# Pooled attention and a GELU MLP on one core: denominators ahead of outputs in the first batch, the last row tile in column parts, and one store per row tile

## The chip, the cores and the metric

The kernel runs on one core of a Trainium2 chip. The metric is the device time of one execution in microseconds (us), lower is better. A profiled execution gives a page and a trace; times inside it are counted from the start of the span.

## The reference

```python
def _attn_ref(q, k, v):                      # 8 batches, 8 heads, 576 rows, 64 columns
    k_p = k.reshape(B, H, Sp, 8, D).mean(axis=3)      # Sp = 72
    v_p = v.reshape(B, H, Sp, 8, D).mean(axis=3)
    scores = scale * np.matmul(q, k_p.transpose(0, 1, 3, 2))
    attn = softmax(scores)
    return np.matmul(attn, v_p)
# heads side by side: x has 4608 rows of 512
h = x @ w_in                                 # 512 -> 2048
g = gelu_tanh(h)
out = g @ w_out                              # 2048 -> 512, float32
```

Keys and values are averaged over eight neighbouring rows, each query row attends over the 72 averaged ones, and a two-layer MLP with a tanh GELU follows.

## The kernel before, in words

**Groups.** The MLP works on nine groups g of 512 rows of x, which is held transposed in xT (128 partitions, 4 slices of the model dimension, 4608 columns). In each group the up-projection `p1_mm` (L336) makes 16 tiles of 128 hidden units by 512 rows in PSUM banks, four matmuls per tile, `gelu` (L342) turns each into a part of gT, and the down-projection `p2_mm` (L345) makes four row tiles of 128 output rows from 16 matmuls each. `store` (L350, L356) copies a row tile from PSUM to an osb buffer (six of them) on VectorE and writes it to memory.

**Order.** The schedule is written by hand: each engine runs its instructions in the order of the program text, and waits are put in where data or buffers demand them. While the group g is in its down-projection, the attention of batch g+1 is woven into it at fixed places (`pos`, in matmuls of the down-projection): `qk` (L239) makes scores, `expo` (L247) their exponentials, `av` (L261) outputs and denominators, `norm` (L268 to L271) reciprocals by a logarithm and an exponential, and `mult` (L279) writes xT. In the up-projection of group g stand the sums for batch g+1: `k_steps` and `v_steps` (L139) on VectorE, the transposes of k (L174), and `v_moves` (L152), two small DMAs on SP's queue that move pooled rows of v from kp to vp.

**Loads.** `load_next` (in group g, for batch g+2) issues the q load on POOL's queue, a DMA transpose of q on SP's queue (L224), then a one-element copy `gate` on POOL (L448) that waits for the transpose, and behind it on POOL the loads of k and v. The weights w_in_b and w_out_b are loaded once; w_out_b in four parts of four hidden blocks fo each, on POOL's queue (L113), behind the loads of batch 1.

**The first batch** has no down-projection to hide in. It stands alone at the start, with steps of its own: `den0` (L289) makes the denominators of two pairs of heads by matmuls with a constant, `inverse0` (L294, L296) their reciprocals into rc0 (two buffers), `av0` (L304) the outputs of two pairs, and `mult0` (L308) their product into xT. c is the half of the rows and pr the first pair of heads. `spin` (L362) issues matmuls of zeros whose results nobody reads. The end of that stage, with PSUM banks as last arguments:

```python
    spin(4, 4)
    av0(0, 0, 4); mult0(0, 0, 4)
    den0(0, 2, 2); inverse0(0, 2, 2)
    av0(1, 0, 0); mult0(1, 0, 0)
    spin(3, 6)
    den0(1, 2, 6); inverse0(1, 2, 6)
    spin(3, 4)
    av0(0, 2, 4); mult0(0, 2, 4)
    spin(3, 0)
    av0(1, 2, 0); mult0(1, 2, 0)
```

Behind it comes the up-projection of group 0, its first eight matmuls on slices 0 and 1 of xT, then those on slices 2 and 3.

**Stores.** The rows of the output that a row tile holds are spread: each run of 32 columns of xT belongs to one of 18 positions within a stride of 18 rows. Each row tile is therefore written by four DMAs of 32 rows of 2 KB, all from SP's queue; the very last row tile uses SP's and ACT's queues in turn. SP's queue in a group holds, in order, the transpose of q, the two moves into vp, and the sixteen stores.

Of the kernel before, what the change touches and what calls it, by code (L numbers as in the profile page):

```python
# [8 lines left out]
F32 = mybir.dt.float32  # L9
# [9 lines left out]
def kernel(  # L19
# [9 lines left out]
    nc = tc.nc  # L29
    B, H, S, D = q.shape  # L30
    Sp = S // 8
    N = B * S
    DM = H * D
    DF = moe_w_in.shape[1]
    KO = DM // 128
    FO = DF // 128
    T = S // 32
    TP = T // 2
    CH = S // 2
    GROUP = 512  # L40
    NG = N // GROUP
# [11 lines left out]
    opool = ctx.enter_context(tc.tile_pool(name="op", bufs=6))  # L53
# [4 lines left out]
    PS = psp.tile([128, 8, 512], F32, name="PS")  # L58
# [19 lines left out]
    def load_v(b, engs):  # L78
        rows = v[b].rearrange("h (j l) d -> j h (l d)", l=8)
        for i in range(2):  # L80
            engs[i % len(engs)].dma_start(out=vts[b % 2][64 * i:64 * i + 64], in_=rows[0:64, 4 * i:4 * i + 4])  # L81

    def load_q(b, i0=0, i1=2):
        if b not in qs:
            qs[b] = qp.tile([128, 2, T * D], BF16, name="qb")
        nc.gpsimd.dma_start(  # L86
            out=qs[b][:, i0:i1],
            in_=q[b].rearrange("(i h) (p t) d -> (h p) i (t d)", i=2, t=T)[:, i0:i1])
# [3 lines left out]
    w_out_b = consts.tile([128, FO, DM], BF16, name="w_out_b")  # L92
# [104 lines left out]
    def trans_k(b, bank):  # L197
        trans_k_mm(b, bank)
        for e in range(2):
            trans_k_copy(b, e, bank)  # L200
# [21 lines left out]
    def trans_q_dma(b):  # L222
        qTs[b] = bp.tile([128, 2, TP, 128], BF16, name="qT")
        nc.sync.dma_start_transpose(out=qTs[b].rearrange("p i t c -> p (i t) c"),  # L224
                                    in_=qs[b].rearrange("p i c -> p (i c)"))
# [6 lines left out]
    def pool_rows(pr):  # L232
        return Sp if pr < PR // 2 else 128
# [49 lines left out]
    def den0(c, pr, bank):  # L283
        for x in range(2):
            e = es[0, c, pr + x]
            n = pool_rows(pr)
            for y in range(2):
                one = ones[:n, pr // 2].rearrange("j a d -> j (a d)")[:, 64 - 64 * y:192 - 64 * y]
                nc.tensor.matmul(out=PS[:, bank + x, :CH], lhsT=one, rhs=e[:n, y, :],  # L289
                                 start=(y == 0), stop=(y == 1))  # L290

    def inverse0(c, pr, bank):
        ld = ep.tile([128, 2, CH], F32, name="ld0", bufs=1)
        nc.scalar.activation(out=ld, in_=PS[:, bank:bank + 2, :CH], func=ACT.Ln)  # L294
        rc = ep.tile([128, 2, CH], F32, name="rc0")
        nc.scalar.activation(out=rc, in_=ld, func=ACT.Exp, scale=-1.0)  # L296
        rcs[0, c, pr] = rc

    def av0(c, pr, bank):
        for x in range(2):  # L300
            e = es.pop((0, c, pr + x))
            n = pool_rows(pr)
            for y in range(2):
                nc.tensor.matmul(out=PS[:, bank + x, :CH], lhsT=window(vz[:n], 2 * (pr + x) + y),  # L304
                                 rhs=e[:n, y, :], start=(y == 0), stop=(y == 1))

    def mult0(c, pr, bank):
        nc.vector.tensor_tensor(out=xT[:, pr:pr + 2, c * CH:(c + 1) * CH], in0=PS[:, bank:bank + 2, :CH],  # L308
                                in1=rcs.pop((0, c, pr)), op=ALU.mult)
# [3 lines left out]
    def act_set(name):  # L313
        nc.scalar.preload_act_table_set(name)  # L314


    def x_bank(g):
        return g % 2
# [9 lines left out]
    def o_bank(g, r):  # L328
        return 1 - x_bank(g) if r % 2 == 0 else x_bank(g)

    gTs = {}
# [9 lines left out]
            gTs[g] = gpool.tile([128, FO, GROUP], BF16, name="gT")  # L341
        nc.scalar.activation(out=gTs[g][:, fo, :], in_=PS[:, h_bank(g, fo), :], func=ACT.Gelu_apprx_tanh)  # L342

    def p2_mm(g, r, fo):
        nc.tensor.matmul(out=PS[:, o_bank(g, r), :], lhsT=gTs[g][:, fo, r * 128:(r + 1) * 128], rhs=w_out_b[:, fo, :],  # L345
                         start=(fo == 0), stop=(fo == FO - 1))

    def store(g, r):
        osb = opool.tile([128, DM], F32, name="osb")
        nc.vector.tensor_copy(out=osb, in_=PS[:, o_bank(g, r), :])  # L350

        for n in range(4):
            b, c = divmod(g * GROUP + r * 128 + n * 32, S)
            rows = out[b * S:(b + 1) * S].rearrange("(p t e) d -> e t p d", t=TP, e=2)
            eng = nc.scalar if (g, r) == (NG - 1, 3) and n % 2 else nc.sync
            eng.dma_start(out=rows[c // CH, c % CH // 32], in_=osb[n * 32:(n + 1) * 32, :])  # L356


    def spin(n, bank):

        for _ in range(n):
            nc.tensor.matmul(out=PS[:, bank, :], lhsT=idle[:, 0:128], rhs=idle, start=True, stop=True)  # L362
# [24 lines left out]
    for h in range(H):  # L387
        i = h // 4
        nc.tensor.matmul(out=PS[64 - 64 * i:72 - 64 * i, 7, h * D:(h + 1) * D],
                         lhsT=identb[0:64, 32 * i + h % 4:32 * i + 32:4], rhs=kps[0][0:64, KR],  # L390
                         start=True, stop=True)
# [3 lines left out]
    for i in range(2):  # L395
        p = slice(64 - 64 * i, 72 - 64 * i)
        nc.vector.tensor_copy(out=vz[p, 4 * i:4 * i + 4, 0],
                              in_=PS[p, 7, 256 * i:256 * i + 256].rearrange("p (h d) -> p h d", d=D))
# [9 lines left out]
    for f in v_steps(0):  # L408
        f()
    inverse0(1, 0, 6)  # L410
    spin(4, 4)
    av0(0, 0, 4)
    mult0(0, 0, 4)
    den0(0, 2, 2)
    inverse0(0, 2, 2)
    av0(1, 0, 0)
    mult0(1, 0, 0)
    spin(3, 6)
    den0(1, 2, 6)
    inverse0(1, 2, 6)  # L420
    spin(3, 4)
    av0(0, 2, 4)
    mult0(0, 2, 4)
    spin(3, 0)
    av0(1, 2, 0)
    mult0(1, 2, 0)
    for t in kps:
# [12 lines left out]
    for g in range(NG):  # L440
        nb = g + 1 if g + 1 < B else None
        act_set(GELU_SET)

        def load_next():

            load_q(g + 2)
            trans_q_dma(g + 2)
            nc.gpsimd.tensor_copy(out=gate, in_=qTs[g + 2][0:1, 1, TP - 1, 0:2])  # L448
            load_k(g + 2, [nc.gpsimd])
            load_v(g + 2, [nc.gpsimd])  # L450

        if 0 < g and g + 2 < B:
            load_next()


        side = {fo: [] for fo in range(FO)}
        if nb is not None:
            kk = k_steps(nb)
            tk = [lambda: trans_k(nb, 4)]
            kk.append(lambda: v_moves(nb))  # L460
            vv = v_steps(nb)
            if g:
                plan = {2: kk[:1], 3: kk[1:], 7: vv[:1], 8: vv[1:], 9: tk}
            else:
                tq = [lambda a=a, i=i: trans_q(nb, *a, (5, 6, 7, 5)[i], nc.vector) for i, a in enumerate(QG)]
                plan = {0: kk, 12: tq[:1], 13: tq[1:2] + tk, 14: tq[2:3], 15: tq[3:] + vv}
            for fo, what in plan.items():
                side[fo] += what

        if g == 0:
            first = [(fo, ko) for ko in (2, 3) for fo in range(4)]
        else:
            late = 3
            rest = [fo for fo in range(4) if fo != late]
            first = [(fo, ko) for ko in range(3) for fo in rest]
            first += [(late, ko) for ko in range(3)]
            first += [(fo, 3) for fo in rest + [late]]
        for fo, ko in first:  # L480
            p1_mm(g, fo, ko)
        for fo in range(FO):
            if fo >= 4:
                for ko in range(KO):
                    p1_mm(g, fo, ko)
            gelu(g, fo)
            for s in side[fo]:
                s()

        if g == 0:  # L490
            load_next()


        todo = {}

        def at(m, f, *a):
            todo.setdefault(m, []).append((f, a))

        if nb is not None:
            act_set(EXP_SET)  # L500
            pos = (6, 14, 20, 27, 34, 41, 48, 55, 61)
            for i in range(len(ORDER) + 1):
                if i < len(ORDER):
                    at(pos[i], qk, nb, *ORDER[i], 2)
                if i:
                    a = (nb, *ORDER[i - 1], 4 + 2 * ((i - 1) % 2))
                    at(pos[i], av, *a)
                if i < len(ORDER):
                    at(pos[i], expo, nb, *ORDER[i], 2)
                if i:  # L510
                    at(pos[i], norm, *a)
                    at(min(pos[i] + 9, 62 if i < len(ORDER) else 65), mult, *a)
        seq = [(r, fo) for r in range(4) for fo in range(FO)]
        if g == 0:

            seq[:32] = [(r, 4 * f4 + f) for f4 in range(4) for r in range(2) for f in range(4)]
        for m, (r, fo) in enumerate(seq):
            for f, a in todo.pop(m, []):
                f(*a)
            p2_mm(g, r, fo)  # L520
            if fo == FO - 1:
                store(g, r)
        for m in sorted(todo):
            for f, a in todo[m]:
                f(*a)


# [28 lines left out]
```

The softmax here doesn't subtract the row's maximum and nothing guards it: scores larger than these inputs give would overflow.

## Time and profile before

| what | us |
|---|---|
| median of 3 runs (lowest, highest) | 309.1 (308.51, 309.18) |
| profiled execution | 308.29 |
| its span | 306.5 |
| TensorE busy | 298.2 |
| ScalarE busy | 219.0 |
| VectorE busy | 150.4 |
| 36 copies to osb, each | 0.69 |
| 142 store issues on SP, each (median) | 0.42 |

The page lists busy time per engine, then the span in 40 slices of 7.66 us with the busy share in tenths, the DMA queues, the chain of waits that ended last, and groups of instructions by line. Queue q0 carries what POOL issues, q1 what SP issues, q10 what ACT issues. A queue's row gives packets, megabytes and the time of its packets as a share of 16 DMA engines. A timeline row gives start, time, engine, line, what is written from what, and in brackets the idle time before it with what ended it.

### The profile page before, as it was taken

The page shows a single profiled execution, that of the slowest core. Times are in us where ns is not written, and L with a number is a line of the kernel's source. Part 1 is how long each engine was busy: PE and PEld are TensorE (multiplying, and loading weights), DVE is VectorE, ACT ScalarE, POOL GpSimd, SP SyncE. Part 2 cuts the span into 40 slices and gives each one's busy share as a digit, 9 for nine tenths or more (in the row PEclk, how much of TensorE's full clock was granted, in tenths as well). Part 3 has the DMA queues.
Part 4 walks back from the last instruction along what each step waited for, and adds up shares of the span by engine and source line. Part 5 has one row for each costly group of instructions (what it writes and reads, how often), then busy time and mean ns, then how long its engine had stood idle before and what let it go on. Part 6 is the DMA issues. An engine that isn't in the chain of part 4 may idle for free.

```text
span 306.5 us, 4325 instructions
## 1 busy us (share of the span) xinstructions
PE 298.2 (97%) x1518; PEld 157.4 (51%) x1548; DVE 150.4 (49%) x334; ACT 219.0 (71%) x402; POOL 36.3 (12%) x69
## 2 busy tenths in 40 slices
PE   8999999999999999999999999999999999999994
PEld 3555555555555555555555555555555555445441
DVE  5868557573677057806681559245933630110021
ACT  1686679868987798779977998789868987206400
POOL 7103002305004000220014000400000000000000
PEclk9999999999999999999999999999999999999999
DMA  7999996987957952596159725662101210121022
GB/s 225 266 257 253 214 186 137 299 176 177 269 146 167 247 122 51 114 282 156 34 112 266 168 56 106 200 151 71 35 1 36 63 41 2 34 70 34 2 70 68
DMA packets 30359, 41.12 MB, mean 134 GB/s; under 512 B 18113, under 2 KB 18113, under 8 KB 29441
## 3 DMA queue, kind: packets, MB, share of 16 engines
q0 software_dynamic: 7856, 25.43, 34.9%
q1 hardware_dynamic: 21888, 14.09, 19.2%
q10 hardware_dynamic: 592, 1.31, 1.2%
q8 instruction: 12, 0.20, 0.3%
q14 instruction: 11, 0.08, 0.1%
HBM read 36.70 MB, written 9.44 MB: 151 GB/s over the span
## 4 chain that ended last, share of the span: by engine, by line
PE 83%; DMA 12%; POOL 1%; issue 1%; ACT 0%; DVE 0%; POOLq 0%
PE PS L345 38%; PE PS L336 36%; DMA kt<-in_k_dram 7%; DMA w_out_b<-in_moe_w_out_dram 5%; PE PS L239 4%; PE PS L261 4%; PE PS L174 1%; POOL w_in_b L105 0%; POOL qb L86 0%; POOL w_out_b L113 0%; DVE osb L350 0%; ACT e L247 0%; ACT ld L269 0%; ACT ld L268 0%; POOL identb masks.py:199 0%
## 5 line engine op out<-in xcount | busy, mean ns | idle before, releaser
L345 PE MATMUL PS<-w_out_b,gT 128*128 128x512 bf16 x560 | 134.2, 379 | 0.9
L336 PE MATMUL PS<-xT,w_in_b 128*128 128x512 bf16 x563 | 126.2, 379 | 0.6
L342 ACT ACTIVATE gT<-PS 128x512 bf16<-128x512 f32 x144 | 81.1, 604 | 47.5 <-PE PS L336 47.4
L336 PEld LDWEIGHTS <-w_in_b 128*128 128x128 bf16 x576 | 64.7, 113 | 57.2
L345 PEld LDWEIGHTS <-gT 128*128 128x128 bf16 x576 | 56.1, 97 | 56.7 <-issue 1.1
L350 DVE COPY osb<-PS 128x512 f32<-128x512 f32 x36 | 24.9, 691 | 98.3 <-PE PS L345 95.3
L279 DVE TENSOR_TENSOR xT<-PS,rc 64x288 bf16<-64x288 f32 x112 | 51.0, 455 | 31.6 <-ACT rc L271 29.3
L247 ACT ACTIVATE e<-PS 72x576 bf16<-72x576 f32 (+1 forms) x64 | 41.0, 646 | 9.1 <-PE PS L239 8.2
L239 PE MATMUL PS<-qT,kT 128*72 128x288 bf16 (+1 forms) x128 | 25.9, 286 | 0.9 <-ACT qT L214 0.6
L271 ACT ACTIVATE rc<-ld 128x288 f32<-128x288 f32 x56 | 24.8, 443 | 1.8
L314 ACT ACT_TABLE_LOAD x17 | 21.8, 1283 | 4.3 <-issue 4.1
L268 ACT ACTIVATE ld<-PS 64x288 f32<-64x288 f32 x56 | 22.8, 407 | 1.3
L269 ACT ACTIVATE ld<-PS 64x288 f32<-64x288 f32 x56 | 22.5, 402 | 1.3
L261 PE MATMUL PS<-e,vp 72*128 72x288 bf16 (+1 forms) x112 | 23.1, 286 | 0.0
L139 DVE TENSOR_TENSOR kt<-kt 128x1280 f32<-128x1280 f32 (+5 forms) x18 | 18.8, 1044 | 5.5 <-DMA kt<-in_v_dram 2.6
L239 PEld LDWEIGHTS <-kT 128*72 128x72 bf16 (+1 forms) x128 | 13.2, 105 | 15.2 <-DVE qT L216 1.2
L448 POOL COPY gate<-qT 1x2 bf16<-1x2 bf16 x6 | 1.0, 174 | 140.0 <-DMA qT<-qb 140.0
L139 DVE TENSOR_TENSOR vt<-vt 128x1024 f32<-128x1024 f32 (+1 forms) x16 | 15.3, 956 | 1.8 <-DMA vt<-in_v_dram 1.5
L184 DVE COPY kT<-PS 64x288 bf16<-64x288 bf16 (+2 forms) x48 | 13.0, 319 | 6.2 <-PE PS L174 6.1
L362 PE MATMUL PS<-idle 128*128 128x512 bf16 x39 | 11.9, 447 | 1.2 <-DVE idle L127 1.2
L261 PEld LDWEIGHTS <-vp 72*128 72x128 bf16 (+1 forms) x112 | 11.0, 98 | 3.8
L81 POOL DMA_DIRECT2D vt<-in_v_dram x14 | 9.0, 655 | 7.5 <-DMA w_in_b<-in_moe_w_in_dram 5.5
(47 smaller groups left out, 90.0 us busy)
## 6 DMA issues: line engine op xcount, KB each, us to landing
out_dram<-osb SPq DMA_DIRECT2D x142, 64.0 KB
kt<-in_k_dram POOLq DMA_DIRECT2D x7, 1024.0 KB, 6.2
vt<-in_v_dram POOLq DMA_DIRECT2D x14, 512.0 KB, 8.6
qb<-in_q_dram POOLq DMA_DIRECT2D x7, 576.0 KB, 11.6
w_in_b<-in_moe_w_in_dram POOLq DMA_DIRECT2D x2, 1024.0 KB, 16.7
w_out_b<-in_moe_w_out_dram POOLq DMA_DIRECT2D x4, 512.0 KB, 13.9
kt<-in_k_dram POOLq DMA_DIRECT2D x7, 128.0 KB, 5.9
kt<-in_v_dram POOLq DMA_DIRECT2D x14, 64.0 KB, 5.7
```

Of the source, the lines that this page charges most:

```text
L139: nc.vector.tensor_tensor(out=o, in0=a, in1=b, op=ALU.add)
L239: nc.tensor.matmul(out=PS[:n, bank + e, :CH].rearrange("j (t p) -> j t p", p=32), lhsT=kTs[b % 2][c][:, h, :n], rhs=qTs[b][:, h // 4, :, h ...
L247: nc.scalar.activation(out=e[:n], in_=PS[:n, bank:bank + 2, :CH], func=ACT.Exp, scale=1.0 / 64.0)
L261: nc.tensor.matmul(out=PS[:, bank + x, :CH], lhsT=window(vps[b % 2][:n], 2 * pr + x), rhs=e[:n, x, :], start=True, stop=True)
L268: nc.scalar.activation(out=ld[0:64], in_=PS[64:128, bank, :CH], func=ACT.Ln)
L269: nc.scalar.activation(out=ld[64:128], in_=PS[0:64, bank + 1, :CH], func=ACT.Ln)
L271: nc.scalar.activation(out=rc, in_=ld, func=ACT.Exp, scale=-1.0)
L279: nc.vector.tensor_tensor(out=xT[rows, pr, col:col + CH], in0=PS[rows, bank + x, :CH], in1=rc[rows], op=ALU.mult)
L336: nc.tensor.matmul(out=PS[:, h_bank(g, fo), c0:c1], lhsT=w_in_b[fo // 8][:, ko, q * 512 + j:(q + 1) * 512:4], rhs=xT[:, ko, r0 + c0:r0 + c ...
L342: nc.scalar.activation(out=gTs[g][:, fo, :], in_=PS[:, h_bank(g, fo), :], func=ACT.Gelu_apprx_tanh)
L345: nc.tensor.matmul(out=PS[:, o_bank(g, r), :], lhsT=gTs[g][:, fo, r * 128:(r + 1) * 128], rhs=w_out_b[:, fo, :], start=(fo == 0), stop=(fo ...
L350: nc.vector.tensor_copy(out=osb, in_=PS[:, o_bank(g, r), :])
```

## The change

It has three parts. In the first batch both remaining `den0`/`inverse0` pairs move ahead of outputs, and the zero matmuls among and ahead of them change from 4 + 3 + 3 + 3 to 2 + 2 + 2: where nine stood between the outputs, two are left, and the four ahead stand in two halves. `store` writes neighbouring runs of 32 rows that belong to the same half of a batch with one DMA of up to 4 x 32 rows, all from SP's queue. The last row tile of the last group is computed in two column parts, 384 and 128 wide, each with its own PSUM bank, copy and store. The built program issues 49 store DMAs where there were 144.

```diff
-    def p2_mm(g, r, fo):
-        nc.tensor.matmul(out=PS[:, o_bank(g, r), :], lhsT=gTs[g][:, fo, r * 128:(r + 1) * 128], rhs=w_out_b[:, fo, :],
-                         start=(fo == 0), stop=(fo == FO - 1))
+    def p2_mm(g, r, fo, bank, c0=0, c1=DM):
+        nc.tensor.matmul(out=PS[:, bank, c0:c1], lhsT=gTs[g][:, fo, r * 128:(r + 1) * 128],
+                         rhs=w_out_b[:, fo, c0:c1], start=(fo == 0), stop=(fo == FO - 1))
+    osbs = {}
-    def store(g, r):
-        osb = opool.tile([128, DM], F32, name="osb")
-        nc.vector.tensor_copy(out=osb, in_=PS[:, o_bank(g, r), :])
-        for n in range(4):
-            b, c = divmod(g * GROUP + r * 128 + n * 32, S)
+    def store(g, r, bank, c0=0, c1=DM):
+        if (g, r) not in osbs:
+            osbs[g, r] = opool.tile([128, DM], F32, name="osb")
+        osb = osbs[g, r]
+        nc.vector.tensor_copy(out=osb[:, c0:c1], in_=PS[:, bank, c0:c1])
+        n = 0
+        while n < 4:
+            b, col = divmod(g * GROUP + r * 128 + n * 32, S)
+            c, t = col // CH, col % CH // 32
+            k = min(4 - n, TP - t)
             rows = out[b * S:(b + 1) * S].rearrange("(p t e) d -> e t p d", t=TP, e=2)
-            eng = nc.scalar if (g, r) == (NG - 1, 3) and n % 2 else nc.sync
-            eng.dma_start(out=rows[c // CH, c % CH // 32], in_=osb[n * 32:(n + 1) * 32, :])
+            nc.sync.dma_start(
+                out=rows[c, t:t + k, :, c0:c1], in_=osb[n * 32:(n + k) * 32, c0:c1])
+            n += k
...
-    spin(4, 4)
+    spin(2, 4)
+    den0(0, 2, 2)
+    inverse0(0, 2, 2)
+    spin(2, 4)
     av0(0, 0, 4)
     mult0(0, 0, 4)
-    den0(0, 2, 2)
-    inverse0(0, 2, 2)
+    den0(1, 2, 6)
+    inverse0(1, 2, 6)
     av0(1, 0, 0)
     mult0(1, 0, 0)
-    spin(3, 6)
-    den0(1, 2, 6)
-    inverse0(1, 2, 6)
-    spin(3, 4)
     av0(0, 2, 4)
     mult0(0, 2, 4)
-    spin(3, 0)
+    spin(2, 0)
     av0(1, 2, 0)
     mult0(1, 2, 0)
...
-        seq = [(r, fo) for r in range(4) for fo in range(FO)]
+        seq = [(r, fo) for r in range(4 if g + 1 < NG else 3) for fo in range(FO)]
...
-            p2_mm(g, r, fo)
+            p2_mm(g, r, fo, o_bank(g, r))
             if fo == FO - 1:
-                store(g, r)
+                store(g, r, o_bank(g, r))
...
+    for c0, c1, bank in ((0, 384, o_bank(g, 3)), (384, DM, 4)):
+        for fo in range(FO):
+            p2_mm(g, 3, fo, bank, c0, c1)
+        store(g, 3, bank, c0, c1)
```

## The prediction

> **What bounds the kernel now.** I read the page's busy times and slices first, then the chain of waits, then the stages the diff touches. All times are us from the span's start.
>
> ```profile
> PE 298.2 (97%) x1518; PEld 157.4 (51%) x1548; DVE 150.4 (49%) x334; ACT 219.0 (71%) x402; POOL 36.3 (12%) x69
> ...
> PEclk9999999999999999999999999999999999999999
> DMA  7999996987957952596159725662101210121022
> ```
>
> TensorE works 97% of the span at full clock, so a change pays only where it shortens TensorE's stream, shortens the tail, or makes TensorE wait. The DMA row is near full over its first six slices (to 46 us) and reaches 9 again in single slices up to 170 us: transfers come in bursts, and early on without a pause. Three places matter.
>
> First, the chain of waits around the first output projection:
>
> ```profile
> 27.46 16.53 DMA w_out_b<-in_moe_w_out_dram
> 43.99 0.04 issue
> 44.03 0.81 PE PS L345 x3
> ```
>
> The last quarter of w_out_b lands at 43.99 and TensorE's matmul on it (fo=12) starts at 44.03. In the trace's starts it is 0.44 behind its predecessor where 0.216 is the pace, and fo=8 was late by 0.22 in the same way. TensorE already waits for this load.
>
> Second, the SP queue in the stage after (timeline: start, time, engine, line), and the matmul it serves in the second group:
>
> ```profile
> 49.86 9.73 SPq L356 DMA_DIRECT2D out_dram<-osb  x16
> 67.40 2.78 SPq L224 DMA_TRANSPOSE qT<-qb  x1
> 70.28 1.42 SPq L152 DMA_DIRECT2D vp<-kp  x2
> ```
> ```profile
> 73.22 0.41 PE L261 MATMUL PS<-e,vp 72*128 72x288 bf16 x2
> ```
>
> SP issues in order. The transpose waits for q of batch 3 (landed 67.35), the two small moves into vp stand behind it, and av reads the first of them at 73.22. Issue 70.28 plus its 0.7 and about 1 to land leaves TensorE some 1 us to spare. This is the thinnest cover in the kernel.
>
> Third, the end:
>
> ```profile
> 302.11 0.69 DVE L350 COPY osb<-PS 128x512 f32<-128x512 f32 x1 [2.76 <-PE PS L345]
> 302.84 0.85 ACTq L356 DMA_DIRECT2D out_dram<-osb  x2
> ```
>
> Copy to 302.80, four stores issued on two queues by 303.7, last data packet at 304.86, span end at 306.5. Profiled time 308.29 = span 306.5 + 1.8; the median of the runs, 309.1, is 0.8 above it.
>
> **What the Trainium skill says.** (1) "DMA: Bandwidth & Descriptors", section "Why a DMA increments its semaphore by 16 and not by 1": a transfer from SP or ACT runs on k engines, the largest k up to 16 that divides the outermost sizes of both sides, the lowest-numbered k, each posting one completion. The trace agrees. ACT's queue in the first 22 us:
>
> ```profile
> q10 hardware_dynamic: 496, 1.18, 14.4%
> ```
>
> Its data packets are 128 (kt, 4 KB), 256 (vt, 2 KB) and 2 x 32 (kt from v, 2 KB) = 448. The other 48 are completions: 16 + 16 for the first two, so 8 each for the two kt loads, whose sides are 32 and 8 long outermost: k = 8, not 16. (2) The same page, "Queues, rings and completion order": each engine takes its rings in turn, and a ring in order. No view here shows one engine alone. (3) "TensorE: Matmul & The Clock Gate", "Back-to-back issue gap": N/2.4 + 2.5 ns; the trace's 0.216 at 512 columns agrees.
>
> **Part by part.**
>
> *First batch.* Nine zero matmuls become two, and both den0/inverse0 move up. Behind the scores (15.98): 2 zeros to 16.41, den(0,2) 4 x 0.123 to 16.90, 2 zeros (kept from the four) to 17.33, av(0,0) to 17.82, den(1,2) to 18.31, av(1,0) to 18.80. Next av(0,2) rewrites the bank that mult(0,0) reads: 17.33 + 0.77 (av to mult in the trace) + 0.76 = 18.86, so 18.93 to 19.42. The two zeros on bank 0 wait for mult(1,0), done 19.84: to 20.33. av(1,2) to 20.82. The up-projection starts at 20.82 for 22.08 now, **1.26 earlier**; 0.25 of the removed 1.51 (7 x 0.216) turns into waits on mult. On ACT, Exp of (0,2) needs the rc0 buffer that mult(0,0) frees, and Ln/Exp of (1,2) queue behind it to 20.97 (now 21.43), so they hold nothing more. But 16 us later TensorE reaches w_out_b 1.26 early, and those loads stand in a DMA stream that is full from 2 us on and that no part of the change speeds up. The fo=12 matmul still starts at 44.03. **Gain 0** (0 to 1.26, the latter if the load came early).
>
> *Stores.* 144 DMAs of 32 rows become 49, most of 4 x 32 rows. Issue time drops (142 x 0.42 = 60 us of SP now), off the path. The built instruction has 4 outermost on the DRAM side and 128 on the other, so by (1) k = 4; a 3 x 32 one runs on 3 engines, a 2 x 32 one on 2, and every one of these loads engine 0 with 64 KB in 32 packets where 8 packets per row tile lie there now. A 2 KB packet costs, from the last 6.5 us (packets, MB, share of 16 engines):
>
> ```profile
> q1 hardware_dynamic: 288, 0.39, 23.2%
> q10 hardware_dynamic: 96, 0.13, 9.0%
> ```
>
> 32.2% x 16 x 6.5 = 33.5 over 256 data packets = 0.13; the packet records show 0.084 where others wait behind. I take 0.09, so 2.9 per store on engine 0.
>
> Does engine 0 have room? The critical stretch starts where the first store can flow (51.3, after the first transpose):
>
> ```profile
> q0 software_dynamic: 848, 2.95, 64.1%
> q1 hardware_dynamic: 1822, 1.31, 30.3%
> ```
>
> From 49.8 to 67.4 the loads cost 64.1% x 17.6 = 11.3 on each engine. Engine 0 gets group 0's stores, 4 x 32 + 2 = 130 packets x 0.09 = 11.7, those loads, and its part of the transpose, 2.8: 25.8, so the vp move behind them ends at 77.1 and lands about 77.5. The av matmul wanted it at 73.22: **TensorE waits 4.2**. Everything on TensorE is queued behind. Ends: 0.084 and 10.5 of loads (their packets at best) give 2.5; 0.126 gives 9. The gate on POOL waits for the transpose too, so k and v of batch 3 come about 5 later than now; v landed 84.67 and the third group's sums want it near 94, which covers that. Later groups put 11 to 15 of stores, 11 of loads and 3 of transposes on engine 0 per 31.8 us, and their vp moves have some 9 us to spare (93.61 against 105.2), so I take 0 there, up to 8 at the high packet price. A wait over 3.4 can halve the clock (the same TensorE page, "What's actually happening"), 0 to 1.7; I take 0. osb has six buffers, 48 us at this pace: hidden.
>
> *Last row tile.* 16 matmuls of 384 (0.1625) and 16 of 128 columns (0.056, the spacing of the 128-column transposes) take 3.50 for 3.46, and the last copy is 128 columns, about 0.29 for 0.69. So the last copy ends at 302.45, not 302.80. The 384-column store is issued at 301.85 (all on SP; ACT's two issues go) and its data may start at 302.65 (0.8 from issue to data now), behind the store of the tile before (on engines 0 to 3 until about 302.95): 32 packets of 1.5 KB at 0.065 (between the 256 B and 2 KB packets' 0.018 and 0.084) to 305.0, then 32 of 512 B at 0.03 to 306.0 against 304.86 now. **Cost 1.2** (0.9 to 3).
>
> Sum: 0 + 4.2 + 1.2 = +5.4: 313.7 against the profiled 308.3, **314.5** against the median.
>
> **Rivals.**
>
> *Stores spread over 16 engines* (the narrow split does not happen). For it: all present stores do spread. Against it: the 48 completions. Then nothing waits in the middle, and the end is issue 302.5 + 0.8 + 0.25 = 303.55 for 304.86: −1.3, **307.8**. It decides at k: with k = 8 the last data end about 304.0 and it is still a gain. Chance 0.10. If w_out_b also came early, 306.6: 0.05.
>
> *Narrow but hidden*: engine 0 drains before the vp move, since it has to be only 4.2 better than my sum; only the tail costs: **310.3**. Chance 0.12.
>
> *Engine 0 becomes the bound*: packets at 0.126 on a shared engine give 17 + 11 + 3 = 31 per group, all of its 31.8, so waits come back in later groups: 9 + 8 + 2, up to **328**, more likely near 321. Chance 0.13.
>
> *Main case*, one wait in the second group: 311.5 to 319. Chance 0.60.
>
> **Numbers.** Likeliest 314.5. A range of 309.5 to 323 leaves out the two gains (0.15) and the far end of the heavy case (0.04). About 0.2% (0.6 us) is what a measurement of this kernel can tell from no change; the gains give faster 0.14, the low edge of the hidden case same 0.04, the rest slower 0.82.
>
> **What the changed profile would show.** The up-projection starting near 20.8 and the fo=12 matmul still at 44.0; an L261 matmul of the second group idle some 4 us behind DMA vp<-kp; the transposes landing late and POOL's gate with them; completions on SP's queue far fewer than 16 per store; an end some 1 us later behind the last copy. I am wrong if stores show 16 completions each, if fo=12 starts at 42.8, or if the vp moves land by 73.

## The result, and the profile after

The changed kernel takes **320.58 us** (median of 4 runs, 319.41 to 321.24) against 308.96 for the kernel before on the same chip (4 runs): ratio 1.0374, 95% interval 1.034 to 1.0408. It is slower, inside the range given, but by 11.6 us where I had forecast 5.4. Its profiled execution took 320.86, of which the span is 318.9 (before: 308.29 and 306.5).

The span is 12.4 longer. Start times of the groups in the two traces place this (a group starts with its first L336 matmul):

| stretch | before | after | difference |
|---|---|---|---|
| to the second group's start | 55.62 | 57.03 | +1.41 |
| its up-projection | 14.09 | 21.84 | **+7.75** |
| from there to the last group's L345 | 218.39 | 218.39 | 0.00 |
| from there to the end of the last copy | 14.70 | 14.35 | −0.36 |
| last copy to the end of the span | 3.69 | 7.31 | **+3.62** |

So there are two places, and seven groups between them that lost nothing. In the page of after, the busy row of TensorE and its clock show the first (40 slices of 8 us; the place is the ninth digit):

```profile
PE   8999899929999999999999999999999999999990
...
PEclk9999999987999999999999999999999999999997
```

The 2 in the ninth slice is a hole where the kernel before had none, and the clock's 8 and 7 in the ninth and tenth are new. The list of waits of after (engine, line, what it waited for: total us, times, longest) names it:

```profile
DVE kt L139 <- DMA kt<-in_v_dram: 9.1, 1, 9.1
PE PS L174 <- DVE kp L139: 5.6, 1, 5.6
PE PS L345 <- DMA w_out_b<-in_moe_w_out_dram: 1.6, 2, 1.3
```

The third line is the wait for w_out_b, longer here than before, where it held the matmuls of fo=8 and fo=12 up by about 0.2 each. The first two are new, and they are not the wait that I had named. TensorE stood before L174, the transpose of the pooled k of batch 2, because VectorE's pooling sums (L139) waited for the tile kt. It is filled by four transfers from POOL's queue: k in a large and a small part, then two small ones from v, and the last of these is what the line names. The timeline of VectorE in after, then of TensorE (start, time, engine, line; in brackets the idle time before it):

```profile
68.51 2.35 DVE L139 TENSOR_TENSOR kt<-kt 128x1280 f32<-128x1280 f32 x2 [9.08 <-DMA kt<-in_v_dram]
70.90 0.49 DVE L139 TENSOR_TENSOR kp<-kt 128x320 bf16<-128x320 f32 x1
```
```profile
71.44 0.71 PE L174 MATMUL PS<-identb,kp 128*128 128x128 bf16 x5 [5.62 <-DVE kp L139]
71.95 7.08 PE L336 MATMUL PS<-xT,w_in_b 128*128 128x512 bf16 x24
```

The same three steps in the kernel before, VectorE and then TensorE:

```profile
60.64 2.35 DVE L139 TENSOR_TENSOR kt<-kt 128x1280 f32<-128x1280 f32 x2 [2.62 <-DMA kt<-in_v_dram]
63.03 0.49 DVE L139 TENSOR_TENSOR kp<-kt 128x320 bf16<-128x320 f32 x1
```
```profile
64.25 0.44 PE L174 MATMUL PS<-identb,kp 128*128 128x128 bf16 x5
64.53 5.13 PE L336 MATMUL PS<-xT,w_in_b 128*128 128x512 bf16 x23
```

There kp was done at 63.52 and TensorE came to it at 64.25: a slack of **0.73**, less than the 1 us that I had taken for the thinnest cover. The last two lines also give the price of the clock: 7.08 for 24 matmuls, 0.295 each, against 5.13 for 23, 0.223. That is 1.7, with the transposes (0.71 for 0.44) 2.0 of the stretch's 7.75, beside 5.78 of waiting, counted from start to start. The granted clock in the trace is 0.50 from 68.64 to 75.46; up to there these matmuls start 0.427 apart, behind it 0.216.

The answer on transfers from 50 to 67 shows how late the load was (KB, then us from issue to landing), before and then after:

```profile
kt<-in_k_dram POOLq DMA_DIRECT2D x1, 1024.0 KB, 6.4
```
```profile
kt<-in_k_dram POOLq DMA_DIRECT2D x1, 1024.0 KB, 12.8
```

The tail is on the timeline of after (the last two copies, and SP's issues):

```profile
305.09 7.10 SPq L362 DMA_DIRECT2D out_dram<-osb  x5
...
310.42 0.56 DVE L354 COPY osb<-PS 128x384 f32<-128x384 f32 x1 [1.91 <-PE PS L345]
311.31 0.29 DVE L354 COPY osb<-PS 128x128 f32<-128x128 f32 x1 [0.34 <-PE PS L345]
```

The two last stores were issued at 311.01 and 311.65 and landed 6.0 and 6.1 us later; in the kernel before, a store landed 1.6 to 2.0 after its issue. Every merged store of 4 row blocks posted 5 semaphore events where a store before posted 16, one of the 5 within 1.1 of the issue and the others when data had landed: k = 4, as forecast.

### The profile page after: what moved, and what is told of

Read it like the earlier page. It is cut to its first block, busy times and chain, and to the rows that moved or that the text cites. A ratio compares the mean times of both kernels' runs of the same rounds, so it can differ in the third digit from the quotient of the medians.

```text
span 318.9 us, 4250 instructions
## 1 busy us (share of the span) xinstructions
PE 301.6 (95%) x1557; PEld 158.4 (50%) x1557; DVE 150.5 (47%) x335; ACT 219.1 (69%) x402; POOL 36.4 (11%) x69
## 4 chain that ended last, share of the span: by engine, by line
PE 75%; DMA 11%; issue 8%; POOL 2%; DVE 1%; POOLq 0%; DVEq 0%
PE PS L345 35%; PE PS L336 32%; DMA kt<-in_k_dram 7%; DMA kt<-in_v_dram 4%; PE PS L261 4%; PE PS L239 4%; DVE kt L139 1%; PE PS L174 1%; POOL qb L86 1%; POOL w_in_b L105 0%; POOL w_out_b L113 0%; POOL kt L76 0%; POOL kt L73 0%; POOL kt L72 0%; DVE kp L139 0%
## 5 line engine op out<-in xcount | busy, mean ns | idle before, releaser
L345 PE MATMUL PS<-w_out_b,gT 128*128 128x512 bf16 (+2 forms) x592 | 136.7, 373 | 1.7 <-DMA w_out_b<-in_moe_w_out_dram 1.6
L336 PE MATMUL PS<-xT,w_in_b 128*128 128x512 bf16 x576 | 129.0, 383 | 0.0
L336 PEld LDWEIGHTS <-w_in_b 128*128 128x128 bf16 x576 | 65.1, 114 | 58.6 <-issue 2.2
L345 PEld LDWEIGHTS <-gT 128*128 128x128 bf16 x592 | 57.0, 97 | 58.1 <-issue 1.7
L354 DVE COPY osb<-PS 128x512 f32<-128x512 f32 (+2 forms) x37 | 25.1, 678 | 99.2 <-PE PS L345 98.9
L139 DVE TENSOR_TENSOR kt<-kt 128x1280 f32<-128x1280 f32 (+5 forms) x18 | 18.8, 1044 | 11.9 <-DMA kt<-in_v_dram 9.1
L139 DVE TENSOR_TENSOR vt<-vt 128x1024 f32<-128x1024 f32 (+1 forms) x16 | 15.3, 956 | 1.7 <-DMA vt<-in_v_dram 1.4
L370 PE MATMUL PS<-idle 128*128 128x512 bf16 x33 | 11.1, 487 | 1.5 <-DVE idle L127 1.2
```

The lines of the kernel that those rows point to most:

```text
L139: nc.vector.tensor_tensor(out=o, in0=a, in1=b, op=ALU.add)
L336: nc.tensor.matmul(out=PS[:, h_bank(g, fo), c0:c1], lhsT=w_in_b[fo // 8][:, ko, q * 512 + j:(q + 1) * 512:4], rhs=xT[:, ko, r0 + c0:r0 + c ...
L345: nc.tensor.matmul(out=PS[:, bank, c0:c1], lhsT=gTs[g][:, fo, r * 128:(r + 1) * 128], rhs=w_out_b[:, fo, c0:c1], start=(fo == 0), stop=(fo ...
L354: nc.vector.tensor_copy(out=osb[:, c0:c1], in_=PS[:, bank, c0:c1])
```

## The experiments

Three theories. **Narrow**: the stores lie on few engines, and that alone costs the time. **Merged**: one long store in place of four short ones costs it, on however many engines. **First batch**: TensorE comes to its loads earlier, or these come later. The first four kernels take the change apart.

### The parts one by one

`e1_first_only`: the kernel before with the first batch's new order alone.

```diff
-    spin(4, 4)
+    spin(2, 4)
+    den0(0, 2, 2)
+    inverse0(0, 2, 2)
+    spin(2, 4)
     av0(0, 0, 4)
...
```

> The first batch's new order alone, stores and last row tile as before. Theory A (the narrow stores cause the whole loss; the first batch's gain ends at the w_out_b wait): the up-projection starts 1.26 after-the-scores earlier, TensorE then waits longer for w_out_b, time 308.5 to 309.2, no change. Theory B (the new order itself makes the loads late: w_out_b's last part landed at 45.4 in the changed kernel, 44.0 before): last part lands near 45.4 again, time about 310.3.

Measured: 308.89 (20 runs), ratio 0.9993 (0.9981 to 1.0006). The up-projection started at 21.02 for 22.08, and the second group at 55.78 for 55.62. The gain is made and is gone 35 us later: the list of waits has 0.9 for w_out_b, where before it names none.

`e2_stores_only`: the merged stores alone, last row tile in one piece.

```diff
-        for n in range(4):
...
+        n = 0
+        while n < 4:
...
+            k = min(4 - n, TP - t)
...
+                out=rows[c, t:t + k], in_=osb[n * 32:(n + k) * 32, :])
+            n += k
```

> Merged stores alone, first batch and last row tile as before. Theory A: the wait of about 5.8 for the pooled k of batch 2 in the second group, some 2 of slowed matmuls behind it, and a longer tail (issue to first data 2.5 for 0.8, then 32 packets on one engine: +3.1): 319 to 321. Theory B: 1.4 less than the changed kernel's loss, and w_out_b's last part at 44.0. A third theory, that it is the first batch together with the stores that makes k of batch 2 late: no wait in the second group, about 312.

Measured: 319.73, ratio 1.0365 (1.0327 to 1.0403). The second group's up-projection took 20.85, with TensorE waiting 4.9 at L174, and the end came 6.96 behind the last copy (3.69 before). The stores carry the loss: 6.75 + 3.27 of the 10.3 by which this span is longer.

`e3_tail_wide`: the last row tile in column parts alone, stores of 32 rows, every second one on ACT's queue as before. `e4_first_tail_wide`: this and the first batch, which is the change without its merged stores. The cut shown is against the changed kernel; `e3_tail_wide` also takes the first batch's order back.

```diff
-            k = min(4 - n, TP - t)
...
+        for n in range(4):
...
+            eng.dma_start(out=rows[c // CH, c % CH // 32, :, c0:c1], in_=osb[n * 32:(n + 1) * 32, c0:c1])
```

> The last row tile in column parts alone, all stores of 32 rows as before (the last tile's eight go to SP and ACT in turn). All theories: the last copy ends 0.35 earlier, four more issues of about 0.42 on two queues take some of it back: 308.2 to 309.0, at best 0.7 below before.

> The changed kernel with its stores back at 32 rows each: first batch and column parts alone. Theory A: the same as the column parts alone, 308.2 to 309.0. Theory B: 1.4 above that, about 310. If it is under 307.8, the first batch's gain came through after all.

Measured: 308.2, ratio 0.9977 (0.9965 to 0.999), and 307.95 (20 runs), ratio 0.9966 (0.9953 to 0.9979). The column parts gain about 0.7 by themselves; with the first batch the kernel beats the changed one and, by 0.2% to 0.5%, the one before. The second group's up-projection took 14.1 in both. The theory of the first batch falls.

### Where the stores cost

`e7_g0_wide`: the changed kernel with group 0's stores at 32 rows.

```diff
-            k = min(4 - n, TP - t)
+            k = min(4 - n, TP - t) if g else 1
```

> The changed kernel, with the stores of group 0 alone back at 32 rows. If the second group's wait comes from group 0's stores in front of the loads of batch 2 (theory A), that wait and the slowed matmuls behind it go, and the tail stays: 311 to 312.5. If narrow stores of later groups also cost, or the wait moves to the third group, 314 or more.

Measured: 311.96, ratio 1.0089 (1.0062 to 1.0116). The second group's up-projection took 14.09, the tail behind the last copy 6.86. Group 0's five merged stores (sixteen here) alone cause the wait at L174.

`e12_ends_wide`: group 0 and the last row tile at 32 rows, merged stores between.

```diff
-            k = min(4 - n, TP - t)
+            k = min(4 - n, TP - t) if g and (g, r) != (NG - 1, 3) else 1
...
-            nc.sync.dma_start(
+            eng = nc.scalar if (g, r) == (NG - 1, 3) and n % 2 else nc.sync
+            eng.dma_start(
```

> The changed kernel with 32-row stores in group 0 and for the last row tile (half of these on the ACT queue as before), and merged narrow stores everywhere between: 66 stores for 49. It asks whether the narrow stores of groups 1 to 8 cost anything. Theory that the loss lies at the two ends only: as the kernel with the first batch and the column parts alone, 308.0 (307.5 to 308.6). If the narrow stores between cost time, through transposes issued late or a last row tile that queues behind them: 309 to 311.

Measured: 309.64, ratio 1.0031 (1.0015 to 1.0048): a miss, above what the theory of the two ends gives. Between the ends it holds: from the second group's start to the last group's L345 it took 232.55, `e4_first_tail_wide` 232.50. The miss is in the tail, 5.45 behind the last copy for 3.55. SP's own waits in this kernel:

```profile
SPq L363 <- DMA out_dram<-osb: 3.4, 3, 2.3
```

The very last store was issued at 305.36, though its data were ready at 302.41. It uses the same semaphore as the merged store of the row tile before, issued at 299.34, which landed 6.0 later. A slow store ahead of the last row tile thus held back a fast one.

### Narrow or merged

Three kernels change the order of columns when GELU writes gT, so that the rows stay in place with another walk of the store: `e5_narrow32` (stores of 32 rows on 4 engines), `e6_merged_wide` (whole row tiles on 16 engines, in the kernel before) and `e8_after_wide` (the same in the changed kernel); row tiles that cross a half of a batch keep four stores in the last two. The lines that these two share are shown; in the first, GELU writes runs of 4 columns that lie 8 apart.

```diff
-        nc.scalar.activation(out=gTs[g][:, fo, :], in_=PS[:, h_bank(g, fo), :], func=ACT.Gelu_apprx_tanh)
+        nc.scalar.activation(out=gTs[g][:, fo, :].rearrange("f (r p t) -> f r t p", p=32, t=4),
+                             in_=PS[:, h_bank(g, fo), :].rearrange("f (r t p) -> f r t p", p=32, t=4), func=ACT.Gelu_apprx_tanh)
...
-            rows = out[b * S:(b + 1) * S].rearrange("(p t e) d -> e t p d", t=TP, e=2)
+            rows = out[b * S:(b + 1) * S].rearrange("(p t e) d -> e p t d", t=TP, e=2)
```

> The kernel before with its 144 stores of 32 rows, but the outermost size of each made 4 (the GELU writes its columns in another order so that the rows still fit). So the number, size and issue of the stores are as before and only the engines are few: 8 packets on each of 4 engines in place of 2 on each of 16. Theory A (few engines): a wait in the second group and a long tail as with merged stores, 315 to 321. Theory C (the merging itself, one large transfer per row tile, does the harm): 308.5 to 309.8.

> The reverse: the kernel before with one store of 128 rows for each row tile that lies in one half of a batch, but 32 as the outermost size on the memory side (the GELU writes row-major within a tile), so 16 engines; the other 12 row tiles keep four stores. Theory A: no wait in the second group, 308.3 to 309.5. Theory C: 315 or more.

> The changed kernel with its merged stores spread over 16 engines as in the merged wide variant: first batch, column parts and one store per row tile. Theory A: no wait, and a tail of one issue for four: 307.0 to 308.2, at or under the first batch with column parts and 32-row stores (307.95). Theory C: 315 or more.

Measured: 535.19 (ratio 1.7307), 359.3 (1.1616) and 357.04 (1.1542): none of the theories had this. The costliest group in the page of `e6_merged_wide`, then of `e5_narrow32` (busy, mean ns of one):

```profile
L342 ACT ACTIVATE gT<-PS 128x512 bf16<-128x512 f32 x144 | 166.6, 1402 | 19.1 <-PE PS L336 19.1
```
```profile
L342 ACT ACTIVATE gT<-PS 128x512 bf16<-128x512 f32 x144 | 324.2, 2714 | 19.1 <-PE PS L336 19.1
```

GELU took 604 ns before and became the bound, so the totals say nothing of the stores. One thing can still be read: near the end of `e6_merged_wide`, a whole row tile of 256 KB on 16 engines landed 2.4 after its issue.

The next three leave GELU alone. What they leave out is the right order of the rows within a store; bytes and addresses are the same. `e9_merged16`: the changed kernel with the 32 rows of a block outermost.

```diff
-            rows = out[b * S:(b + 1) * S].rearrange("(p t e) d -> e t p d", t=TP, e=2)
+            rows = out[b * S:(b + 1) * S].rearrange("(p t e) d -> e p t d", t=TP, e=2)
...
-                out=rows[c, t:t + k, :, c0:c1], in_=osb[n * 32:(n + k) * 32, c0:c1])
+                out=rows[c, :, t:t + k, c0:c1], in_=osb[n * 32:(n + k) * 32, c0:c1])
```

> The changed kernel with every merged store walked in the other order: the outermost count is the 32 pixels, not the 2 to 4 row blocks, so that it spreads over 16 engines. Same number of stores (49), same bytes, same addresses; the order of the rows within a row tile is left wrong, nothing else differs, and no other engine has a different instruction. Narrowness theory: the second group's wait is gone and the last stores land about 2.4 us after their issue, as such stores did with the permuted GELU, so 308.0 (307.3 to 309.0), the kernel with the first batch and the column parts alone being at 307.95. Merging theory (one long store instead of four short ones is what hurts, on however many engines): the wait stays and the tail stays long, 316 to 321. If only the tail is from narrowness: about 317.

Measured: **307.66**, ratio 0.9965 (0.9948 to 0.9982). The same 49 stores on 16 engines cost nothing. The page now has a landing time, since 16 completions come:

```profile
out_dram<-osb SPq DMA_DIRECT2D x23, 256.0 KB, 2.4
```

and the load of k for batch 2 is back to its old length (transfers from 50 to 67):

```profile
kt<-in_k_dram POOLq DMA_DIRECT2D x1, 1024.0 KB, 5.7
```

The theory that merging costs on however many engines falls here: nothing but the walk of the stores differs, and 12.9 us go. The walk changes two things at once, the number of engines and the order of the addresses.

`e10_narrow32`: the kernel before, 144 stores of 32 rows, each walked as 4 x 8, so on 4 engines. `e11_half32`: as 8 x 4, on 8.

```diff
-            eng.dma_start(out=rows[c // CH, c % CH // 32], in_=osb[n * 32:(n + 1) * 32, :])
+            eng.dma_start(out=rows[c // CH, c % CH // 32].rearrange("(i a) d -> a i d", a=4), in_=osb[n * 32:(n + 1) * 32, :])
```

> The kernel before with its 144 stores of 32 rows, each walked as 4 x 8 rows, so that each lies on 4 engines; nothing merged; the order of the rows within each 32 is left wrong. Narrowness theory: engines 0 to 3 get the same 32 packets for each row tile as in the changed kernel, so the second group waits as long (5 to 8 us with the slow clock after it), and the tail grows by about 0.8 us only, since a store of 8 packets on an engine landed 2.5 us after its issue against 1.7: 314 to 318. Merging theory: within 1 us of before, 308.5 to 310.

> As the last one, but each store walked as 8 x 4 rows, on 8 engines. Narrowness theory with a dose: the chain on each engine is half as long, 16 packets for each row tile, and the slack of 0.7 us takes the rest: a wait of 1 to 3 us in the second group, 309.5 to 312.5. If the loads only starve while stores are queued without a gap, and 8 engines drain between row tiles, no wait: 308.8 to 309.5. Merging theory: 308.5 to 309.5.

Measured: 317.63, ratio 1.0285 (1.0254 to 1.0317), and 309.67 (20 runs), ratio 1.0026 (1.0015 to 1.0037). So narrowness costs without merging. 8 engines are nearly enough: the wait of 1 to 3 expected for them did not come (14.09 in the second group), and only the tail grew, 4.43 for 3.69. The two walks touch the same 32 rows in different orders too, so no run takes the order of the addresses apart from the number of engines; that the time follows the number of completions, 4, 8 or 16, speaks for the engines.

How `e10_narrow32` loses its time is telling, for the wait is another one. SP's timeline in it, then TensorE's:

```profile
71.66 4.46 SPq L224 DMA_TRANSPOSE qT<-qb  x1
76.21 1.44 SPq L152 DMA_DIRECT2D vp<-kp  x2
```
```profile
78.43 0.66 PE L261 MATMUL PS<-e,vp 72*128 72x288 bf16 x2 [3.88 <-DMA vp<-kp]
```

Here k of batch 2 took 7.9 us to land and cost TensorE about 0.6; q of batch 3 landed at 71.60 (67.35 before), the transpose and the vp moves queued behind it on SP, and av waited 3.9. This is the wait of my prediction, at its place and near its size (4.2), in a kernel that is not the changed one. Its span is 9.2 longer than before: 0.5 to the second group's start, 0.6 in its up-projection, 5.7 in this wait and the slow clock behind it, and 2.4 in the tail, where 0.8 was expected.

The time from issue to landing of that 1 MB load of k orders the kernels that leave GELU alone, by how group 0 is stored: 5.7 (`e9_merged16`) to 6.4 (before) on 16 engines, 5.9, which is no longer, on 8, 7.9 on 4 with short stores, 12.4 (`e2_stores_only`) and 12.8 (after) on 4 with merged ones. Merging does no harm on 16 engines; on 4 it makes the delay of this load three to four times as large. The whole times lie closer, as the short narrow stores lose theirs at the later wait: 10.6 above before for `e2_stores_only`, 8.8 for `e10_narrow32`.

## Why the prediction was right and wrong

**First batch, gain 0: right.** From the end of the scores to the up-projection my walk gives 4.84; all seven kernels with the new order took 4.83, all others 6.1. The start itself, forecast 20.82, was 21.54 in after, whose scores ended at 16.71 for 15.98. And w_out_b takes the gain back: the list of waits of after has it at 1.6, and `e1_first_only` ends within 0.1% of before. The +1.41 of the first row of the table is this load stream too: the last part of w_out_b landed at 45.40 in the profiled run of after and between 43.75 and 45.85 in the others, though no store is issued before 49.7. From that landing to the second group's start it is 11.63 in after as in before.

**Stores on 4 engines: right**, with the place, the second group. The rule of the Trainium skill, "DMA: Bandwidth & Descriptors", section "Why a DMA increments its semaphore by 16 and not by 1", agrees with the walks tried: an outermost count of 4 or 8 gave 4 or 8 completions beside the one at issue, and one of 32 gave 16. The rival in which the stores spread over 16 engines is refuted for the changed kernel, and `e9_merged16` shows that its worked-out time was good: 307.8 forecast, 307.66 measured. The rival in which narrow stores stay hidden falls with the 7.75 of the second group.

**The wait of 4.2 at the vp move: the step that failed.** I held the work on the shared engines against one deadline only, the last, which I called the thinnest cover. A thinner one lay ahead of it. The tile kt of batch 2 is the first load to run beside group 0's stores, and the pooled k made from it had 0.73 to spare, which was to be read from the two timelines shown above. Counted from the issue of k, kt was complete after 14.8 for 8.3: 6.5 more, of which 0.73 was slack and 5.8 became waiting.

The wait that I had named was then covered by this one. In after the data of the first vp move were down at 81.72, and TensorE came to av at 82.38. Without the loss at L174 it would have come near 74.6 and waited about 7 there; this is an estimate from these starts, and no run shows it. So the sum of engine 0's work was too low as well: it had the move down at 77.5, or 78.9 with the 1.41 by which the stage began late.

What the sum lacked is in the packet records. I took 0.09 for a store's packet, and added loads and stores as if it did not matter in which order an engine takes them. In after the first packet of k ran 3.2 after its issue (1.3 before and in `e10_narrow32`). Until then, from 52.5 on, no load's packet ran, and the stores' 140 packets still took 216 ns on average, where 84 is their pace later. From its first packet to its last, k then took 8.8 (4.2 before, 5.3 in `e10_narrow32`). The same page's section "Queues, rings and completion order" says that each engine takes its rings in turn; no view shows one engine alone, so how much of this the turns explain is open.

In `e10_narrow32`, with short stores, the load fared better, the later deadline was the one that broke, and the 4.2 came out as 3.9. That it came so near is in part luck: the move was down 0.9 later than forecast, and TensorE came 1.3 later.

**The clock, taken as 0: wrong by about 2.** I had an estimate of 0 to 1.7 for it from the Trainium skill, "TensorE: Matmul & The Clock Gate", section "What's actually happening", where the clock halves after an idle window of about 3.4 us. The trace agrees that an idle stretch halves the clock: the granted share fell to 0.50 at 68.64, 2.8 after TensorE had gone idle, and was 1 again at 75.46, 4.0 after it had begun again. A wait must be priced with what follows it: 5.78 + 1.97 = 7.75.

**Later groups, 0: right.** 218.39 in both, although SP's issue of a transpose took 9.1 at 98.89 (2.7 before). The rival in which engine 0 becomes the bound is refuted.

**Last row tile, cost 1.2: right in sign, short by 2.1.** The last copy ended 0.36 earlier (forecast 0.35). But the term behind it was mis-sized. I had the first data 0.8 after issue, from the short stores, and the store before this one out of the way 3.6 after its issue. The merged narrow ones show their first packet 1.2 after issue and land 5.7 to 6.2 after it. Three of these follow each other, by the rule above on the same four engines, and the end moved by +3.62 − 0.36 = 3.3.

So of the error of 6.2 between forecast (5.4) and result (11.6), 3.5 are the second group (7.75 for 4.2: 1.6 of waiting, 2.0 of clock), 2.1 the tail, and 0.6 are left. That is less than the 1.41 by which the load stream of the profiled run was late; how much of that the median holds is not shown.

## What to carry to other kernels

When transfers move to fewer engines, list every load that shares those engines in that window, in the order of their deadlines, and read the slack of each from the timeline of its consumer; here the first to break was not the one with the most work queued before it, and it covered the later one. Merge stores only so that the outermost counts of both sides still give 16 engines: the same 49 stores cost 12.9 us in one order of their walk and nothing in the other. Near the end of a kernel take the time from issue to landing from a transfer of the same shape, and let no slow store share a semaphore with the last one.

## What was unexpected of the hardware

- A merged store on 4 engines starts slowly. A lone one in after, issued at 301.63, had its first packet at 302.83 and brought 16 of its 128 packets until 304.1, some of them of 420 to 930 ns. From 305.1 on it was at 24 each half microsecond, of 84 ns. On 16 engines (`e9_merged16`, issued at 292.98) 128 packets were through 0.8 after the first. Why the start is slow is not settled.
- Why a load starts so late and gets so little beside merged stores, and fares so much better beside short ones, stays open too; no run takes the two queues apart.
- GELU's time depends on how its bf16 output is walked: 604 ns for 128 x 512 written in order, 1402 in steps of 8 bytes, 2714 in runs of 4 elements that lie 16 bytes apart. The input was read in order in each. Three kernels show this, and why is open.
